# The stretch ahead of the main loop, put in another order: band, weights, conversion, gathers

## The chip, the cores and the metric

The kernel runs on one NeuronCore of a Trainium2 chip. The metric is the device time of one execution in microseconds (us). The time before is 1235.25 us, the median of three runs (1234.21 to 1237.3). The engines are named as in the profile: PE (TensorE, matmuls), PEld (its weight loads), DVE (VectorE), ACT (ScalarE), POOL (GpSimd) and SP (SyncE, which here only issues DMAs). ACT and POOL issue DMAs too, in the order of their own programs; the issuing parts are called SPq and ACTq in the trace.

## The reference

For x of shape (8, 4224, 192) in float32, cut to what matters:

```python
w = softmax(weight, axis=-1)                       # 8 heads x 7 taps
x = einsum('hk,bskhg->bshg', w, causal windows of x)   # a 7-tap convolution along the sequence
u = x + real(fft(fft(x, axis=1), axis=2))          # sequence 4224 = 33 * 128, features 192
un = (u - mean(u)) / sqrt(var(u) + 1e-6)           # over the 192 features
out = u + maximum(un @ w_ch1, 0) @ w_ch2           # 192 -> 768 -> 192, weights in float64
```

The two weight matrices arrive as 64-bit floats, so the kernel itself turns their 8-byte words into 32-bit floats.

## The kernel before, in words

**Values in two parts.** All large products are made of float16 pairs: a high part (ACT, one copy with a scale) and a low part (DVE, what is left). The scale of each operand is a power of two from its norm: ACT squares and sums, PE adds over the partitions (`pn`), ACT takes a root, DVE a reciprocal and a mask (`pow2_of_norm`).

**Stages of one batch.** (1) Convolution: PE multiplies windows `xt` of the input by a banded matrix `band` made from the taps (`conv_unit`, L472), ACT copies the result to `xa`, and DMAs store it to a scratch array `sc` in DRAM. (2) The rows come back from `sc` in another order as `xs` (for batch 0 by four indirect gathers on POOL, L572; later by plain DMAs) and are split into `XH` (ACT, L605 in batch 0) and `XL` (DVE, L612 in batch 0). (3) Stage A, a transform of length 128 (PE, L659, 16 tiles `pa`, each copied as `yh` by ACT, L667, and `yl` by DVE, L668). (4) Stage B, 33 by 3 (PE `pb`, L685; ACT and DVE make `V`, L693 and L694). (5) For each of nine groups of 512 rows (`it`), `prep`: the last transform (`pq`, L755), the row itself gathered into `xr` (`load_res`, L723, on POOL in batch 0), sum, mean and variance, `un`, its split `hl`, and a DMA transpose `kt`. (6) The MLP: `ph` (L892, six tiles), `hh` and `hlo` (ACT L896, DVE L897), `po` (L911, L914, L917), then the sum and the store.

**The loop and what stands ahead of it.** From `keep_order(tc)` on, a loop over 72 steps (8 batches of 9 groups) runs steps 5 and 6 and, as fill, stages 1 to 4 of the batches that follow. The change lies ahead of it, in about a hundred lines that carry batch 0 up to its first groups, make the convolution of batch 1, and prepare the weights. Each engine runs its instructions in the order in which they were recorded, so an instruction that waits holds all that stand behind it on that engine, DMA issues included.

**Names that the change touches.**
- `make_band`, `load_band` (L206 to L234): DVE works out the softmax of the taps, SP writes them as one row to DRAM (`line_d<-back`, L226), and reads it back shifted for each partition (`band_runs<-line_d`, L230); DVE copies it to `band` in eight pieces (L234). The first convolution matmul needs all of it.
- `load_group` (L493): an input chunk of batch 0 in two or three DMAs. Chunks 0 and 1 are issued by ACT; chunks 2 to 5 by SP.
- `from_float64` (L270 to L300): eight bytes to a float32, ten DVE instructions for each of four pieces: `w1a`, `w1c` (the first weight matrix W1) and `w2_0`, `w2_1` (the second, W2). `some(convs[k], n)` records the next n of them.
- `load_raw2(i)` (L323): loads half i of W2; half 0 into the memory of `XL`, half 1 (`raw_w2_1`) into a buffer of the tag `xs`, which is free once the first gathered piece is split.
- `high1`, `low1` (L371 to L388): W1's high parts on ACT (three instructions), its low parts on DVE (three, and two copies). `split2`: the same for W2. `square_w` (L342) and `pow2_of_norm`: their scales `s_w`.
- `c16_sb`: constants. `F` (128 columns twice) is used by stage A, `R` by stage B, `G` by `pq`.
- `gathers(k)`: four gathers on POOL of one group's rows into `xr`, of which there are three buffers.

## Time and profile before

| | us |
|---|---|
| three runs | 1234.21, 1237.3, 1235.25 |
| median | 1235.25 |
| the profiled execution | 1241.18 |
| its span, first to last instruction | 1239.4 |
| PE busy in the span | 1172.8 |
| first `ph` matmul on PE | 101.83 |

The profile is one execution, with its own time, which is 5.9 us above the median of the runs; durations come from it. Times in rows are counted from the span's start. A row of the time line gives start, length, engine, line, operation, output and input, shape, count, and in brackets how long the engine was idle before it and what ended that. A row of the groups gives line, engine, operation, shape and count, then busy time and mean length of one in ns, then the idle time before. A row of the table by windows gives the stretch, its length, the busy time and instruction count of PE, PEld, DVE, ACT and POOL, the granted PE clock (1.00 is full), the DMA share and GB/s. PE is busy for 95% of the span; the idle part lies for the most part ahead of 140 us.

### The profile page before, as it was taken

The page shows a single profiled execution, that of the slowest core. Times are in us where ns is not written, and L with a number is a line of the kernel's source. Part 1 is how long each engine was busy: PE and PEld are TensorE (multiplying, and loading weights), DVE is VectorE, ACT ScalarE, POOL GpSimd, SP SyncE. Part 2 cuts the span into 40 slices and gives each one's busy share as a digit, 9 for nine tenths or more (in the row PEclk, how much of TensorE's full clock was granted, in tenths as well). Part 3 has the DMA queues.
Part 4 walks back from the last instruction along what each step waited for, and adds up shares of the span by engine and source line. Part 5 has one row for each costly group of instructions (what it writes and reads, how often), then busy time and mean ns, then how long its engine had stood idle before and what let it go on. Part 6 is the DMA issues. An engine that isn't in the chain of part 4 may idle for free.

```text
span 1239.4 us, 30189 instructions
## 1 busy us (share of the span) xinstructions
PE 1172.8 (95%) x12234; PEld 933.0 (75%) x12234; DVE 807.2 (65%) x1998; ACT 818.6 (66%) x1581; POOL 501.1 (40%) x503
## 2 busy tenths in 40 slices
PE   5278899999999999999999999999999999999999
PEld 4276578787878878787877878788787867777777
DVE  4787575567666666667566676666865786556654
ACT  5476686678657876678656886578665676556542
POOL 2428233355244444445333552444443452346210
PEclk9599999999999999999999999999999999999999
DMA  8856784695435853486535754358452442323321
GB/s 261 316 149 150 163 207 133 171 215 149 108 100 155 211 139 79 120 204 174 136 93 157 190 149 109 96 150 207 108 126 78 122 90 68 78 68 87 74 53 46
DMA packets 225732, 170.14 MB, mean 137 GB/s; under 512 B 119151, under 2 KB 206925, under 8 KB 225592
## 3 DMA queue, kind: packets, MB, share of 16 engines
q1 hardware_dynamic: 212646, 141.03, 45.1%
q0 software_dynamic: 11136, 25.34, 7.0%
q8 instruction: 95, 1.56, 0.5%
q10 hardware_dynamic: 1810, 1.84, 0.5%
q14 instruction: 45, 0.37, 0.1%
HBM read 84.50 MB, written 58.50 MB: 115 GB/s over the span
## 4 chain that ended last, share of the span: by engine, by line
PE 78%; DVE 9%; ACT 5%; DMA 4%; issue 2%; another core or an unknown queue 1%; SPq 1%; POOL 1%; ACTq 0%; DVEq 0%
PE ph L892 30%; PE po L911 9%; PE po L917 9%; PE po L914 9%; PE pa L659 7%; PE pq L755 5%; PE pc L472 5%; PE pb L685 5%; DMA sc<-xa 2%; ACT un L835 1%; DVE XL L637 1%; DVE hlo L897 1%; ACT XH L633 1%; ACT hh L896 1%
## 5 line engine op out<-in xcount | busy, mean ns | idle before, releaser
L892 PE MATMUL ph<-kt,W 128*128 128x512 f16 (+1 forms) x2160 | 494.2, 362 | 9.9 <-DVE hlo L897 7.2
L897 DVE SCALAR_TENSOR_TENSOR hlo<-ph,hh 128x512 f16<-128x512 f32 (+1 forms) x400 | 271.1, 679 | 251.0 <-ACT hh L896 220.2
L896 ACT ACTIVATE hh<-ph 128x512 f16<-128x512 f32 (+1 forms) x400 | 237.2, 594 | 290.3 <-PE ph L892 266.9
L911 PE MATMUL po<-W,hh 128*128 128x192 f16 x1584 | 388.2, 246 | 2.7 <-ACT hh L896 1.7
L914 PE MATMUL po<-W,hh 128*128 128x192 f16 x1584 | 388.1, 246 | 2.2 <-DVE W L394 2.2
L917 PE MATMUL po<-W,hlo 128*128 128x192 f16 x1584 | 388.0, 247 | 1.5 <-DVE hlo L897 1.4
L892 PEld LDWEIGHTS <-W 128*128 128x128 f16 x2160 | 193.5, 98 | 153.1 <-issue 12.6
L791 POOL TENSOR_TENSOR u<-u,xr 128x768 f32<-128x768 f32 (+1 forms) x70 | 119.1, 1702 | 319.6 <-ACT u L790 286.1
L723 POOL DMA_INDIRECT xr<-sc,rows_sb x175 | 193.2, 1104 | 50.5 <-issue 34.8
L849 POOL TENSOR_TENSOR hl<-un,hl 128x512 f16<-128x512 f32 (+1 forms) x144 | 126.1, 898 | 145.9 <-ACT hl L846 120.4
L911 PEld LDWEIGHTS <-hh 128*128 128x128 f16 x1584 | 155.2, 98 | 19.7 <-ACT hh L896 2.2
L917 PEld LDWEIGHTS <-hlo 128*128 128x128 f16 x1584 | 154.9, 98 | 17.8 <-issue 2.6
L914 PEld LDWEIGHTS <-hh 128*128 128x128 f16 x1584 | 155.1, 98 | 16.4 <-issue 0.7
L668 DVE SCALAR_TENSOR_TENSOR yl<-pa,yh 99x512 f16<-99x512 f32 x128 | 86.6, 686 | 66.9 <-ACT yh L667 48.4
L835 ACT ACTIVATE un<-u,nm,y 128x192 f32<-128x192 f32 x256 | 119.5, 544 | 8.0 <-DVE nm L822 5.3
L659 PE MATMUL pa<-c_sb,XH 128*128 128x128 f16 x1024 | 105.5, 222 | 16.7 <-ACT XH L605 16.1
L472 PE MATMUL pc<-xt,band 128*120 128x144 f32 x756 | 109.3, 289 | 4.8 <-DVE V L694 3.4
L472 PEld LDWEIGHTS pc<-xt,band 128*120 128x120 f32 x756 | 100.4, 184 | 13.4 <-DVE V L694 3.8
L659 PEld LDWEIGHTS <-XH 128*128 128x128 f16 x1024 | 84.9, 104 | 28.4 <-ACT XH L605 16.2
L923 DVE SCALAR_TENSOR_TENSOR u<-po,fo,u 128x384 f32<-128x384 f32 (+1 forms) x136 | 80.6, 593 | 37.8 <-PE po L917 29.2
L637 DVE SCALAR_TENSOR_TENSOR XL<-xs,s_x,XH 128x768 f16<-128x768 f32 (+1 forms) x56 | 100.4, 1796 | 6.0 <-ACT XH L633 6.0
L755 PE MATMUL pq<-c_sb,V 128*128 128x130 f16 (+1 forms) x1440 | 96.6, 215 | 2.5 <-issue 2.5
(145 smaller groups left out, 1498.0 us busy)
## 6 DMA issues: line engine op xcount, KB each, us to landing
out_dram<-u SPq DMA_DIRECT2D x64, 384.0 KB
xt<-in_xw_dram SPq DMA_DIRECT2D x36, 576.0 KB
sc<-xa SPq DMA_DIRECT2D x33, 540.0 KB
xs<-sc SPq DMA_DIRECT2D x84, 192.0 KB
xs<-sc SPq DMA_DIRECT2D x28, 216.0 KB
xr<-sc SPq DMA_DIRECT2D x56, 96.0 KB
xt<-in_xv_dram SPq DMA_DIRECT2D x6, 504.0 KB
sc<-xa SPq DMA_DIRECT2D x6, 472.5 KB
```

The lines of the kernel that those rows point to most:

```text
L472: nc.tensor.matmul(pc[:WR, h - h0], band[:, h], xt[:, :, h * GRP : (h + 1) * GRP], start=True, stop=True,)
L659: nc.tensor.matmul(pa[:, i], x[:, at], F[:, l], start=(n == 0), stop=(n == 2))
L723: nc.gpsimd.indirect_dma_start(bt.xr[it][:, g], None, bt.sc[: S if b else 128 * LP], bass.IndirectOffsetOnAxis(ap=(rows_sb if b else lines ...
L755: nc.tensor.matmul(po, weights(v, ND * r + k3), rhs[:, 0] if it == Q0 else rhs, start=(r + n == 0), stop=(r == 1 and n == 2),)
L835: nc.scalar.activation(un[:, g], u[:, g], AF.Identity, bias=nm[:, g : g + 1], scale=y[:, g : g + 1],)
L849: nc.gpsimd.tensor_tensor(bl[:, :, o : o + n], un[:, :ng, f], hi[:, :, f], op=ALU.subtract)
L892: nc.tensor.matmul(ph[:, n], W1[:, w, ht * 128 : (ht + 1) * 128], kt[:, k], start=(i == 0), stop=(i == len(order) - 1),)
L896: anchor[0] = nc.scalar.activation(hh, ph, AF.Relu).ins
L897: anchor[1] = nc.vector.scalar_tensor_tensor(hlo, ph, 0.0, hh, op0=ALU.max, op1=ALU.subtract).ins
L911: nc.tensor.matmul(po[:, g % 2], hh[:, ht, tk], W2[:, ht, 0], start=(ht == 0), stop=False)
L914: nc.tensor.matmul(po[:, g % 2], hh[:, ht, tk], W2[:, ht, 1], start=False, stop=False)
L917: nc.tensor.matmul(po[:, g % 2], hlo[:, ht, tk], W2[:, ht, 0], start=False, stop=(ht == 5),)
```

## The change

What it does, all of it ahead of the loop:
- **Band.** Input chunk 2 is issued by ACT behind chunks 0 and 1; the load of `band_runs` follows directly on the store of its row on SP.
- **W2 and constants.** Half 0 of W2 and `F` are issued by ACT behind the last of its stores; half 1 of W2 now stands ahead of `R`, `G` and the row numbers, and all of these behind the fourth split on SP.
- **Conversion.** Eight DVE instructions in place of ten: the sign is kept by one combined instruction, and the last three bits of the low word are dropped by one shift.
- **W1.** `high1` and `low1` now stand ahead of the splits of batch 0, the pieces of the W2 conversion between the low parts; the square of W2's half 0 goes behind stage B.
- **Gathers.** The rows of group 2 are gathered with those of groups 0 and 1; those of group 3 in two pairs; the four of group 4 between these.
- **Order of the rest.** The conversion of `w2_1`, its norm, `split2` and the stages of `prep` of groups 0 and 1 are recorded earlier and mixed otherwise.

ACT, from its last stores to its splits; `sc` is the scratch array, `XL` here the landing place of half 0 of W2, `c_sb` the constants, `W` the split W1. Before:

```order
L959 DMA sc_173<-xa_5_287 112x2x192
L959 DMA sc_173<-xa_5_287 120x2x192
L255 ACTIVATE r_x_331<-r_x_331 128x1
L342 ACTIVATE sq_w_0_350,nrm_w_349<-w1a 128x768
L342 ACTIVATE sq_w_1_352,nrm_w_349<-w1c 128x384
L255 ACTIVATE r_w_361<-r_w_361 128x1
L605 ACTIVATE XH<-xs_0_341,s_x_335 128x2x432 x2
L605 ACTIVATE XH<-xs_1_343,s_x_335 128x2x384 x2
```

ACT at the same place, now:

```order
L955 DMA sc_173<-xa_5_285 112x2x192
L955 DMA sc_173<-xa_5_285 120x2x192
L326 DMA XL<-in_w_dram 128x3x384
L1090 DMA c_sb<-in_c_dram 128x256
L255 ACTIVATE r_x_327<-r_x_327 128x1
L338 ACTIVATE sq_w_0_346,nrm_w_345<-w1c 128x384
L338 ACTIVATE sq_w_1_348,nrm_w_345<-w1a 128x768
L255 ACTIVATE r_w_354<-r_w_354 128x1
L367 ACTIVATE W_78<-w1a,s_w_358 128x768
L370 ACTIVATE W_78<-w1c,s_w_358 64x384 x2
L601 ACTIVATE XH<-xs_0_337,s_x_331 128x2x432 x2
```

Two DMA issues stand ahead of the roots and squares now, and three copies of W1 ahead of the splits; before, those copies stood behind the last split.

DVE, from the scale of W1 to the first low split of batch 0 (`cv` are the buffers of the conversion, `w2f` its result). Before:

```order
L257 RECIPROCAL r_w_361<-r_w_361 128x1
L259 TENSOR_SCALAR s_w_368<-r_w_361 128x1
L262 TENSOR_SCALAR s_w_368<-s_w_368 128x1
L292 SCALAR_TENSOR_TENSOR XL<-XL,cv_w_0_315 128x576
L294 TENSOR_TENSOR cv_w_0_314<-cv_w_0_314,XL 128x576
L297 TENSOR_SCALAR cv_w_0_315<-XL 128x576
L299 SCALAR_TENSOR_TENSOR w2f<-cv_w_0_315,cv_w_0_314 128x576
L612 SCALAR_TENSOR_TENSOR XL<-xs_0_341,s_x_335,XH 128x432 x4
```

DVE at the same place, now:

```order
L262 TENSOR_SCALAR s_w_358<-s_w_358 128x1
L279 TENSOR_SCALAR cv_w_0_312<-XL 128x576
L281 SCALAR_TENSOR_TENSOR cv_w_0_312<-XL,cv_w_0_312 128x576
L285 TENSOR_SCALAR cv_w_0_313<-cv_w_0_312 128x576
L380 SCALAR_TENSOR_TENSOR W_78<-w1c,s_w_358,W_78 64x384
L384 COPY W_78<-W_78 64x2x384
...
L375 SCALAR_TENSOR_TENSOR W_78<-w1a,s_w_358,W_78 128x768
L291 TENSOR_TENSOR cv_w_0_312<-cv_w_0_312,XL 128x576
L293 TENSOR_SCALAR cv_w_0_313<-XL 128x576
L295 SCALAR_TENSOR_TENSOR w2f<-cv_w_0_313,cv_w_0_312 128x576
L608 SCALAR_TENSOR_TENSOR XL<-xs_0_337,s_x_331,XH 128x432 x4
```

Before, six of the ten conversion instructions stood ahead of the scale and four behind it; now the whole conversion and all low parts of W1 stand between the scale and the first split.

POOL, behind the first eight gathers of rows (`xr`, one row for each group of rows; `hl` is the split of `un`). Before:

```order
L849 TENSOR_TENSOR hl_0_870<-un_0_855,hl_0_870 128x4x64
L723 DMA xr_2_874<-sc_173,lines_sb 128x192 x4
L700 COPY V_0_708<-V_2_938 128x12x8
L849 TENSOR_TENSOR hl_1_970<-un_1_933,hl_1_970 128x4x128
L849 TENSOR_TENSOR hl_1_970<-un_1_933,hl_1_970 128x4x64
L723 DMA xr_3_974<-sc_173,lines_sb 128x192 x4
L723 DMA xr_4_1205<-sc_173,lines_sb 128x192 x4
L791 TENSOR_TENSOR u_2_1006<-u_2_1006,xr_2_874 128x768
```

POOL at the same place, now:

```order
L719 DMA xr_2_428<-sc_173,lines_sb 128x192 x4
L696 COPY V_0_709<-V_0_675 128x12x8
L696 COPY V_0_709<-V_1_711 128x12x8
L719 DMA xr_3_813<-sc_173,lines_sb 128x192 x2
L719 DMA xr_4_1197<-sc_173,lines_sb 128x192 x4
L845 ISA
L845 TENSOR_TENSOR hl_0_872<-un_0_862,hl_0_872 128x4x128
L845 TENSOR_TENSOR hl_0_872<-un_0_862,hl_0_872 128x4x64
L719 DMA xr_3_813<-sc_173,lines_sb 128x192 x2
L696 COPY V_0_709<-V_2_940 128x12x8
```

Group 2 is fetched ahead of stage B now, and the eight gathers that stood in one run behind `hl_1` are gone from there.

The diff, with the lines of smaller moves left out:

```diff
@@ from_float64
-        V.tensor_scalar(ai, hi_w, 30, 30, op0=SR, op1=SL)
         V.tensor_scalar(bi, hi_w, 5, 2, op0=SL, op1=SR)
-        V.tensor_tensor(bi, bi, ai, op=ALU.bitwise_or)
-        V.scalar_tensor_tensor(bi, lo_w, 29, bi, op0=SR, op1=ALU.bitwise_or)
-        V.tensor_scalar(lo_w, lo_w, 3, 3, op0=SL, op1=SR)
+        V.scalar_tensor_tensor(
+            bi, hi_w, 0xC0000000, bi, op0=ALU.bitwise_and, op1=ALU.bitwise_or
+        )
         V.tensor_scalar(ai, bi, 23, 23, op0=SR, op1=SL)
-        V.scalar_tensor_tensor(rem, lo_w, 2.0 ** -52, aux, op0=ALU.mult, op1=ALU.mult)
+        V.tensor_scalar(lo_w, lo_w, 1, None, op0=SR)
+        V.scalar_tensor_tensor(rem, lo_w, 2.0 ** -51, aux, op0=ALU.mult, op1=ALU.mult)
...
-    for ch in range(2):
+    for ch in range(3):
         load_group(first, ch, nc.scalar, *slots[ch])
     make_band()
-    load_group(first, 2, nc.sync, *slots[2])
+    load_band()
...
     for store in late:
         store()
-    load_raw2(0)
-    nc.sync.dma_start(c16_sb[:, n_r : n_r + n_f], c16[:, n_r : n_r + n_f])
+    load_raw2(0, nc.scalar)
+    nc.scalar.dma_start(c16_sb[:, n_r : n_r + n_f], c16[:, n_r : n_r + n_f])
...
     norm = pow2_of_norm(mlp["nw1"], 2, 11, "w1")
     next(norm)
+    next(norm)
+    mlp["s1"] = last(norm)
+    high1()
     some(convs[2], 3)
-    next(norm)
+    low1(0)
+    low1(1)
+    some(convs[2], 2)
+    low1(2)
     some(convs[2], 3)
-    mlp["s1"] = last(norm)
-    some(convs[2], 4)
...
         if n == 3:
+            load_raw2(1, nc.sync)
             nc.sync.dma_start(c16_sb[:, :n_r], c16[:, :n_r])
...
-            load_raw2(1)
...
     low()
-    high1()
-    square_w("w2", mlp["w2_0"], 0)
-    for f in gathers(0) + gathers(1):
+    for f in gathers(0) + gathers(1) + gathers(2):
         f()
...
+    square_w("w2", mlp["w2_0"], 0)
     chunk(second, 0)
     prep_piece(1)
+    prep_piece(0)
+    later = gathers(3)
+    for f in later[:2]:
+        f()
...
     total()
-    stage_b(first, 3)
-    some(half, 3)
-    chunk(second, 5)
-    stage_b(first, 4)
     square_w("w2", mlp["w2_1"], 1)
     norm = pow2_of_norm(mlp["nw2"], 2, 15, "w2")
+    stage_b(first, 3)
+    chunk(second, 5)
     next(norm)
+    stats.pop(0)()
+    stage_b(first, 4)
     next(norm)
+    mlp["s2"] = last(norm)
     for f in stats:
         f()
-    mlp["s2"] = last(norm)
```

More of the change, by code (lines that the diff above doesn't have):

```diff
@@ L277, in from_float64 @@
         bi, ai = bits.bitcast(U32), aux.bitcast(U32)
-        V.tensor_scalar(ai, hi_w, 30, 30, op0=SR, op1=SL)
-        yield
         V.tensor_scalar(bi, hi_w, 5, 2, op0=SL, op1=SR)
         yield
-        V.tensor_tensor(bi, bi, ai, op=ALU.bitwise_or)
-        yield
-        V.scalar_tensor_tensor(bi, lo_w, 29, bi, op0=SR, op1=ALU.bitwise_or)
-        yield
-        V.tensor_scalar(lo_w, lo_w, 3, 3, op0=SL, op1=SR)
+        V.scalar_tensor_tensor(
+            bi, hi_w, 0xC0000000, bi, op0=ALU.bitwise_and, op1=ALU.bitwise_or
+        )
         yield
@@ L291, in from_float64 @@
         yield
-        V.scalar_tensor_tensor(rem, lo_w, 2.0 ** -52, aux, op0=ALU.mult, op1=ALU.mult)
+        V.tensor_scalar(lo_w, lo_w, 1, None, op0=SR)
+        yield
+        V.scalar_tensor_tensor(rem, lo_w, 2.0 ** -51, aux, op0=ALU.mult, op1=ALU.mult)
         yield
@@ L321, in load_raw1, with load_raw2 @@
             )
-    def load_raw2(i):
+    def load_raw2(i, queue):
         w2v = w2.rearrange("(c p) e -> p c e", p=128)
@@ L329, in load_raw2 @@
             to = raw("w2_1", "xs", 3 * D)
-        nc.sync.dma_start(
+        queue.dma_start(
             to.rearrange("p (c e) -> p c e", c=3), w2v[:, 3 * i : 3 * i + 3]
@@ L1062 @@
     nc.sync.dma_start(wt, weight.rearrange("(o h) k -> o (h k)", o=1))
-    for ch in range(2):
+    for ch in range(3):
         load_group(first, ch, nc.scalar, *slots[ch])
     make_band()
-    load_group(first, 2, nc.sync, *slots[2])
+    load_band()
     nc.scalar.activation(cp.tile([128, 1], F32, name="warm"), eps, AF.Sqrt)
-    load_band()
     for ch in range(3, NCH):
@@ L1093 @@
         store()
-    load_raw2(0)
-    nc.sync.dma_start(c16_sb[:, n_r : n_r + n_f], c16[:, n_r : n_r + n_f])
+    load_raw2(0, nc.scalar)
+    nc.scalar.dma_start(c16_sb[:, n_r : n_r + n_f], c16[:, n_r : n_r + n_f])
     convs.append(convert("w2_0", 3 * D))
-    some(convs[1], 10)
     norm = scales(first)
+    some(convs[1], 4)
     next(norm)
+    some(convs[1], 4)
     next(norm)
@@ L1103 @@
         load_x(first, i)
-    square_w("w1", mlp["w1a"], 0)
-    square_w("w1", mlp["w1c"], 1)
+    square_w("w1", mlp["w1c"], 0)
+    square_w("w1", mlp["w1a"], 1)
     norm = pow2_of_norm(mlp["nw1"], 2, 11, "w1")
     next(norm)
+    next(norm)
+    mlp["s1"] = last(norm)
+    high1()
     some(convs[2], 3)
-    next(norm)
+    low1(0)
+    low1(1)
+    some(convs[2], 2)
+    low1(2)
     some(convs[2], 3)
-    mlp["s1"] = last(norm)
-    some(convs[2], 4)
     low = None
@@ L1144 @@
     prep_piece(1)
+    prep_piece(0)
     chunk(second, 1)
-    for _ in range(3):
-        prep_piece(0)
-    for part in range(2):
-        conv_unit(second, 2, part)
     prep_piece(0)
-    for f in gathers(2):
-        f()
-    conv_unit(second, 2, 2)
+    conv_unit(second, 2, 0)
+    prep_piece(0)
     transposes(first, 0)
-    for _ in range(2):
-        prep_piece(1)
-    for i in range(3):
-        low1(i)
     half = convert("w2_1", 3 * D)
-    chunk(second, 3)
+    some(half, 1)
     for _ in range(3):
         prep_piece(1)
+    for part in range(1, 3):
+        conv_unit(second, 2, part)
+    for f in later[2:]:
+        f()
+    some(half, 2)
+    prep_piece(1)
+    chunk(second, 3)
+    prep_piece(1)
     stage_b(first, 2)
     prep_piece(1)
-    for f in gathers(3):
-        f()
+    some(half, 2)
+    transposes(first, 1)
     some(half, 1)
-    transposes(first, 1)
-    some(half, 4)
     chunk(second, 4)
```

## The prediction

> **What bounds the kernel now.** I read the table by windows first: length, busy time and count of PE, PEld, DVE, ACT and POOL, granted PE clock, DMA share, GB/s.
>
> ```profile
> span 1239.4 us, 30189 instructions
> 13.94:40.51 26.57, 13.46 (x100) 12.84 (x100) 16.82 (x42) 13.39 (x30) 6.10 (x9) 0.81 0.90 284
> 40.51:53.88 13.37, 0.00 (x1) 0.01 (x1) 8.96 (x19) 5.61 (x7) 10.63 (x10) 0.50 0.86 312
> 53.88:70.12 16.24, 14.33 (x194) 13.75 (x194) 13.93 (x22) 13.45 (x23) 2.92 (x3) 0.88 0.64 247
> 70.12:101.83 31.71, 25.82 (x321) 24.64 (x322) 26.89 (x73) 23.80 (x51) 15.94 (x16) 0.95 0.66 164
> 101.83:122.44 20.61, 16.16 (x134) 11.05 (x134) 14.61 (x42) 12.00 (x28) 16.62 (x19) 0.92 0.58 153
> 122.44:140.00 17.56, 12.56 (x98) 8.11 (x96) 11.41 (x32) 9.21 (x14) 8.23 (x9) 0.99 0.48 99
> 140.00:1239.40 1099.40, 1086.97 (x11381) 859.52 (x11381) 709.34 (x1745) 735.87 (x1423) 440.44 (x435) 1.00 0.51 129
> ```
>
> From 140 on PE is idle for 1099.40 - 1086.97 = 12.4 us of 1099, so a shift of the loop's start arrives whole at the end, and nothing in the loop can repay more. Ahead of 140 PE is idle for 13.4 us while batch 0 is fetched and split (40.51 to 53.88), then 1.9, 5.9, 4.5 and 5.0 us in the next windows. The change can only act there.
>
> The time line next (start, length, engine, line, operation, and the idle time before with what ended it) gives the order of events up to the first matmul with a low part:
>
> ```profile
> 6.95 0.84 SPq L493 DMA_DIRECT2D xt<-in_xw_dram  x2
> 7.83 0.42 SPq L230 DMA_DIRECT2D band_runs<-line_d  x1
> 13.62 1.53 DVE L234 COPY band<-band_runs 128x120 f32<-128x120 f32 x8 [6.96 <-DMA band_runs<-line_d]
> 31.75 3.27 ACTq L959 DMA_DIRECT2D sc<-xa  x2
> 35.25 0.20 ACT L255 ACTIVATE r_x<-r_x 128x1 f32<-128x1 f32 x1 [5.67 <-DVE r_x L254]
> 37.56 0.46 DVE L279 TENSOR_SCALAR cv_w<-XL 128x576 uint32<-128x576 uint32 x1 [0.46 <-DMA XL<-in_w_dram]
> 40.51 1.22 POOL L572 DMA_INDIRECT xs<-sc,lines_sb  x1 [11.26 <-DVE cv_w L285]
> 43.15 0.76 DVE L299 SCALAR_TENSOR_TENSOR w2f<-cv_w,cv_w 128x576 f32<-128x576 uint32 x1
> 46.86 2.41 DVE L612 SCALAR_TENSOR_TENSOR XL<-xs,s_x,XH 128x432 f16<-128x432 f32 x4 [2.95 <-ACT XH L605]
> 54.53 0.33 PE L659 MATMUL pa<-c_sb,XL 128*128 128x128 f16 x1 [0.22 <-DVE XL L612]
> ```
>
> The gather comes at 40.51, DVE waits 2.95 us for the first high part, and PE starts when the low parts are there. The releaser printed for the gather, a DVE line, had long been done; what ends that wait is a DMA, the last store.
>
> **The change, part by part.** *Band.* Two issues (0.84 us) leave SP ahead of the band's load, and chunk 2's data flows earlier, while the DMA engines are nearly idle:
>
> ```profile
> 6.00:8.00 2.00, 0.00 (x0) 0.00 (x0) 0.59 (x3) 1.77 (x3) 0.00 (x0) 1.00 0.19 61
> ```
>
> The band load takes 13.62 - 7.83 = 5.8 us from issue to first copy, behind chunk 2's transfer. At the lower bound it gains nothing (DMA full anyway: 0.90 up to 40.51), at the upper 0.84 plus some 1.4 of that queueing, -2.2. I take -1.0, nearest to the issue row.
>
> *Last stores and gather.* W2's half 0 and F go behind the last stores on ACT. Of the window before the gather at most the stretch from W2's landing can be saved, 40.51 - 37.56 = 2.95, and the band's 1.0 to 2.2 with it: -1 to -5; I take -4. The first high split would come 4 us earlier with it, but that does not set the end any more, because DVE has other work then.
>
> *DVE ahead of the low splits.* The conversion of half 0 ran from 37.56 to 43.91. Two kinds of instruction go from it:
>
> ```profile
> L283 DVE TENSOR_TENSOR cv_w<-cv_w,cv_w 128x576 uint32<-128x576 uint32 x1 | 0.8, 757 | 0.0
> L281 DVE TENSOR_SCALAR cv_w<-XL 128x576 uint32<-128x576 uint32 x1 | 0.5, 451 | 0.0
> ```
>
> That is 1.2 us; without the scale's three small ones (0.5) it is 6.35 - 0.5 - 1.2 = 4.7 us. The low parts of W1, five instructions, come from the stretch behind stage B:
>
> ```profile
> 84.51 0.74 DVE L384 SCALAR_TENSOR_TENSOR W<-w1c,s_w,W 64x384 f16<-64x384 f32 x1
> 87.10 1.02 DVE L379 SCALAR_TENSOR_TENSOR W<-w1a,s_w,W 128x768 f16<-128x768 f32 x1
> L612 DVE SCALAR_TENSOR_TENSOR XL<-xs,s_x,XH 128x384 f16<-128x384 f32 (+1 forms) x16 | 8.9, 626 | 4.3 <-ACT XH L605 4.3
> ```
>
> From 84.51 to 87.10 + 1.02 they take 3.6 us. So DVE has 4.7 + 3.6 = 8.3 us of work ahead of its first low split, from the landing of W2 and the scale of W1 on. Both I put near 37.6: W2 is issued about 2 us later than before but with less in its way; the scale needs ACT's root (35.25), which now stands behind two more DMA issues but behind a shorter wait for the stores (3.27 in the row). First low split: 37.6 + 8.3 = 45.9, before 46.86. Eleven splits of 0.626 (6.9 us) lead to the first matmul with a low part: 52.8 to 53.0 in place of 54.53. **Term 1: -1.5.** If W2 lands a microsecond earlier or later, so does all of this: bounds -3 to +4 (the third rival). The 2.4 us that W1's own two conversions lose count for nothing: ACT's root and squares cover them, being held by the issues; without that cover they would add to the gain.
>
> *ACT in stage A.* ACT made W1's high parts and a square between its last split and the first `yh`:
>
> ```profile
> 55.39 0.92 ACT L371 ACTIVATE W<-w1a,s_w 128x768 f16<-128x768 f32 x1
> 57.47 0.69 ACT L342 ACTIVATE sq_w<-w2f 128x576 bf16<-128x576 f32 x1
> 58.15 2.04 ACT L667 ACTIVATE yh<-pa 99x512 f16<-99x512 f32 x4
> 58.76 11.31 DVE L668 SCALAR_TENSOR_TENSOR yl<-pa,yh 99x512 f16<-99x512 f32 x16 [1.64 <-ACT yh L667]
> ```
>
> These 2.8 us are gone from there. DVE's sixteen `yl`, 11.31 us without a gap, then set the end of stage A; the 1.64 us that they waited can go, but DVE itself comes free only at 45.9 + 16 x 0.626 = 55.9 and behind that needs a first `yh`. I take half a microsecond beyond term 1. **Term 2: -0.5**, bounds 0 to -1.6.
>
> *Gathers on POOL.* Group 2's four go ahead of stage B, where POOL is busy for 2.92 of 16.24 us: nothing. Six more stand ahead of `hl_0` now, behind which all of group 0 waits.
>
> ```profile
> L723 POOL DMA_INDIRECT xr<-sc,rows_sb x175 | 193.2, 1104 | 50.5 <-issue 34.8
> 83.68 2.10 POOL L849 TENSOR_TENSOR hl<-un,hl 128x512 f16<-128x512 f32 x2 [9.58 <-ACT hl L846]
> ```
>
> Six at 1.1 us and 0.3 of issue are 8.4 us; POOL was idle for 9.58 there. I count nothing, with +0.5 as a bound, since four of them also wait for group 1's sum to free their buffer.
>
> *From stage B to the first `ph`.* DVE sheds the 3.6 us of low parts, two instructions of W2's second half, one of them slow there, and a wait:
>
> ```profile
> L283 DVE TENSOR_TENSOR cv_w<-cv_w,cv_w 128x576 uint32<-128x576 uint32 x1 | 1.6, 1598 | 0.0
> 80.66 0.18 DVE L817 RECIPROCAL y<-sd 128x4 f32<-128x4 f32 x1 [1.63 <-ACT sd L813]
> ```
>
> That is 3.6 + 1.6 + 0.5 + 1.6 = 7.3 us of 31.71, but DVE is idle for 31.71 - 26.89 = 4.8 us there, PE for 5.9, and ACT's 23.80 us, conversion copies among them, are neither shorter nor better placed. **Term 3: -2**, between 0 (ACT holds the pace) and -5.9 (all idle time of PE).
>
> *W2 ready earlier.* PE waits once for W2's low part, and the clock falls behind that; a like wait stands ahead of a convolution.
>
> ```profile
> 90.81 0.75 PE L472 MATMUL pc<-xt,band 128*120 128x144 f32 x4 [3.07 <-DVE V L694]
> 90.00:95.00 5.00, 4.19 (x47) 4.17 (x48) 4.90 (x8) 4.62 (x10) 4.53 (x6) 0.70 0.54 158
> 116.00 0.32 PE L914 MATMUL po<-W,hh 128*128 128x192 f16 x1 [2.17 <-DVE W L394]
> 115.00:120.00 5.00, 4.00 (x24) 3.34 (x24) 4.76 (x9) 2.32 (x6) 3.75 (x5) 0.66 0.25 60
> ```
>
> The conversion and the norm of the second half are recorded earlier, so the 2.17 us go, and with them part of the loss at 0.66 (5 us at full clock would do 1.7 us more; I take half). **Term 4: -3**, bounds 0 (W2 is late in another place) and -3.9. The Trainium skill ("TensorE: Matmul & The Clock Gate", Part 1: The HAM clock gate) speaks against the second half of this: the clock halves only after an idle window of about 3.4 us, so a gap of 2.17 would cost no clock. The trace shows 0.66 behind it, and 0.70 behind a gap of 3.07, both shorter than the page's window. By the page term 4 would be -2.2 and the sum 0.8 smaller; I go by the rows.
>
> Sum: -1.5 - 0.5 - 2 - 3 = -7.0. Against the profiled execution's own 1241.18 us (span 1239.4 and 1.8 around it) that is 1234.2. That execution lies 5.9 us above the median of the runs, so I subtract from the median: 1235.25 - 7.0 = 1228.2, said as **1228**.
>
> **Rivals.** *First: it gives more.* The chain of waits has two steps that no engine explains:
>
> ```profile
> 102.56 4.00 another core or an unknown queue
> 125.04 4.96 another core or an unknown queue
> ```
>
> In both, POOL is amid eight gathers in a row. Nowhere else in the run do eight stand together, and the change parts them. If the gathers make these stalls, what PE still loses there goes too: 4.5 - 2.2 (term 4) in 101.83 to 122.44 and 5.0 up to 140, in all 7.3, which gives 1235.25 - 14.3 = 1221. Against it: the profiled execution was 5.9 us above the median, so the stalls may be a matter of that execution alone. Chance 0.18.
>
> *Second: the gain is hidden.* The order of transfers changes little, W2 decides as late as before, and what is shed behind stage B was cover for ACT's copies (23.80 of 31.71) and for PE's waits on PSUM. Then terms 1 and 2 stand with -2 and the rest gives nothing: 1233, within 0.3% (3.7 us, about what a measurement of this kernel can tell from no change). That the whole does not do what it says, because the band's row and not its load is late, ends here as well. For it: ACT has no more slack than DVE. Against: the wait of 2.17 names W2. Chance 0.20.
>
> *Third: slower, W2's half 0 lands late.* It stands behind ACT's last stores, whose issue ended at 31.75 + 3.27 = 35.0, and the conversion and all low parts of W1 stand behind it ahead of every low split.
>
> ```profile
> 31.34 6.20 DMA XL<-in_w_dram
> 45.15 7.72 DMA xs<-sc,lines_sb
> ```
>
> Before, it took 6.20 us; beside gathers, which took up to 7.72, it would land at 35.0 + 7.7 = 42.7, and the first low split would start at 42.7 + 8.3 = 51.0, +4.2. With half a microsecond won by ACT stage A ends 3.7 us later; half 1 of W2 stands on SP behind the fourth split and is late with it, so terms 3 and 4 give nothing: 1235.25 + 3.7 = 1239. It decides from a landing later than 46.86 - 8.3 = 38.5 on. Against it: fewer bytes are ahead of the stores than before, so they should end sooner than 35.0. Chance 0.12.
>
> **How the numbers follow.** My own case has 0.50, with -4 to -10 (1225 to 1231). With the first rival that makes 0.68 for faster by over 0.3%; the second gives 0.20 for no change, the third 0.12 for slower. The range for 8 in 10 reaches from 1219 (the first rival with its bounds) to 1236 (the second with +0.5 on POOL and a term 1 of nothing), which leaves out the third rival and the tails.
>
> **What would show it.** Right: band copies near 11.7 to 12.6 in place of 13.62; the gather at 36 to 38; conversion from about 37.6 and the first low split at about 45.9; the first matmul with a low part at 53; `yl` without the 1.64 us of idle time; no wait for `W` near 116 and a clock above 0.66 behind it; first `ph` near 98, and 7 us off at the point that was 140. Wrong: W2 landing past 38.5, DVE waiting ahead of its conversion, POOL's `hl_0` behind a gather, or PE as idle between 70 and 122 as before. If the two stalls of 4.00 and 4.96 us are gone and the time is near 1221, the first rival holds.

## The result, and the profile after

| | before | after |
|---|---|---|
| median, us | 1235.25 (7 runs, 1233.18 to 1237.30) | 1224.65 (7 runs, 1221.33 to 1229.70) |
| ratio to before | 1 | 0.9924 (95%: 0.9908 to 0.9940) |
| profiled execution: its time, its span | 1241.18, 1239.4 | 1224.36, 1222.5 |
| first matmul with a low part | 54.53 | 51.88 |
| first `pb` (stage B) | 69.40 | 66.31 |
| first `ph` | 101.83 | 96.03 |
| first output store issued | 134.13 | 120.05 |

The change saves 10.6 us by the medians, 0.6 to 0.9% by the interval; 7.0 were forecast. The two profiled executions differ by 16.8, more than the medians, because that of before lay 5.9 above its own median. In the rows of after all line numbers behind the conversion are 4 lower (L608 is the low split that was L612). Its table by windows, cut at the same events as before (band, gather, first `pa`, second row of `pb`, first `ph`, and 125.92, which answers to 140):

```profile
13.42:37.50 24.08, 13.46 (x100) 12.84 (x100) 11.74 (x33) 13.49 (x30) 6.50 (x9) 0.82 0.89 298
37.50:50.62 13.12, 0.00 (x0) 0.00 (x0) 12.80 (x25) 7.65 (x10) 10.58 (x9) 0.50 0.80 279
50.62:67.03 16.41, 14.46 (x194) 13.95 (x194) 14.81 (x24) 11.18 (x18) 10.15 (x7) 0.84 0.88 330
67.03:96.03 29.00, 24.57 (x273) 23.64 (x274) 23.74 (x68) 23.32 (x50) 18.27 (x19) 0.90 0.70 182
96.03:125.92 29.89, 29.78 (x300) 22.18 (x298) 25.31 (x70) 24.86 (x50) 18.82 (x21) 0.99 0.71 184
125.92:1222.50 1096.58, 1083.64 (x11363) 857.88 (x11360) 710.88 (x1747) 735.33 (x1418) 439.49 (x435) 1.00 0.51 128
```

PE's 13.4 us without work while batch 0 is fetched and split are still there (13.12), only sooner. From stage B to the first `ph` PE is idle for 4.4 us in place of 5.9. The large difference is the stretch behind the first `ph`: 0.1 us of idle time, before 4.5 and 5.0 in its two windows. The first events, from the time line:

```profile
13.10 1.51 DVE L234 COPY band<-band_runs 128x120 f32<-128x120 f32 x8 [6.45 <-DMA band_runs<-line_d]
32.45 0.41 ACTq L326 DMA_DIRECT2D XL<-in_w_dram  x1
37.50 1.07 POOL L568 DMA_INDIRECT xs<-sc,lines_sb  x1 [7.51 <-DMA XL<-in_w_dram]
37.99 0.46 DVE L279 TENSOR_SCALAR cv_w<-XL 128x576 uint32<-128x576 uint32 x1
45.02 0.78 DVE L295 SCALAR_TENSOR_TENSOR w2f<-cv_w,cv_w 128x576 f32<-128x576 uint32 x1
45.73 8.74 DVE L608 SCALAR_TENSOR_TENSOR XL<-xs,s_x,XH 128x432 f16<-128x432 f32 x16
51.88 0.33 PE L655 MATMUL pa<-c_sb,XL 128*128 128x128 f16 x1 [0.82 <-DVE XL L608]
```

From 37.99 on DVE has no idle time at all: 7.7 us of conversion and low parts, then sixteen low splits in 8.74 without a gap, where before they came in three pieces and waited for ACT.

```profile
53.53 0.61 ACT L663 ACTIVATE yh<-pa 99x512 f16<-99x512 f32 x1 [1.30 <-DVE XL L608]
57.27 9.71 DVE L664 SCALAR_TENSOR_TENSOR yl<-pa,yh 99x512 f16<-99x512 f32 x13 [0.19 <-ACT yh L663]
```

ACT is free before there is anything to copy in stage A (1.30 us idle); the copies of W1 that stood there are gone. For the end of W2's preparation, POOL's sum of group 2 and W2's high part on ACT, and then PE's longest waits between 60 and 140 (view of the waits: in all, times, longest):

```profile
90.30 2.43 POOL L787 TENSOR_TENSOR u<-u,xr 128x768 f32<-128x768 f32 x1 [0.35 <-ACT u L786]
101.18 0.77 ACT L389 ACTIVATE W<-w2f,s_w 128x576 f16<-128x576 f32 x1
```

```profile
PE pc L468 <- ACT XH L473: 2.1, 1, 2.1
PE pc L468 <- DVE V L690: 1.8, 1, 1.8
```

No wait for `W` is left, and no stretch that no engine explains.

### The profile page after: what moved, and what is told of

Same layout as the page of the kernel before. It is cut to its first block, busy times and chain, and to the rows that moved or that the text cites. A ratio compares the mean times of both kernels' runs of the same rounds, so it can differ in the third digit from the quotient of the medians.

```text
span 1222.5 us, 30180 instructions
## 1 busy us (share of the span) xinstructions
PE 1169.4 (96%) x12234; PEld 933.6 (76%) x12234; DVE 804.6 (66%) x1990; ACT 821.0 (67%) x1581; POOL 504.0 (41%) x503
## 4 chain that ended last, share of the span: by engine, by line
PE 82%; DVE 7%; ACT 4%; DMA 4%; issue 2%; POOL 1%; SPq 0%; ACTq 0%; DVEq 0%
PE ph L888 31%; PE po L907 9%; PE po L913 9%; PE po L910 9%; PE pa L655 7%; PE pc L468 6%; PE pq L751 5%; PE pb L681 5%; ACT un L831 1%; DVE XL L633 1%; DMA sc<-xa 1%; DMA xt<-in_xw_dram 1%; DVE hlo L893 1%; ACT XH L629 1%; ACT hh L892 1%
## 5 line engine op out<-in xcount | busy, mean ns | idle before, releaser
L719 POOL DMA_INDIRECT xr<-sc,rows_sb x175 | 193.2, 1104 | 50.5 <-issue 34.8
L655 PE MATMUL pa<-c_sb,XL 128*128 128x128 f16 x512 | 95.3, 221 | 0.8 <-DVE XL L608 0.8
```

What stands on the lines that cost most here:

```text
L655: nc.tensor.matmul(pa[:, i], x[:, at], F[:, l], start=(n == 0), stop=(n == 2))
L719: nc.gpsimd.indirect_dma_start(bt.xr[it][:, g], None, bt.sc[: S if b else 128 * LP], bass.IndirectOffsetOnAxis(ap=(rows_sb if b else lines ...
```

## The experiments

Twelve kernels in three sets of four. The sets ran on three different chips, each with its own runs of before beside it (medians 1235.77, 1234.36 and 1241.66 us), so ratios are compared, not times. After has its own ratio from the result above and ran beside none of the sets. The events are from one profile of each kernel, and one profile says only so much: e7 and e12 have after's order behind stage B, yet take 31.6 and 30.1 us from `pb` to `ph` where after takes 29.7, so differences of up to 2 us in that column decide nothing. "Store" is the first output store. The expectations give 70.12 as the first `pb` of before, which is its second row; the first is at 69.40. The order in which an engine runs comes out of a scheduler that starts from the recorded one (so `xr_4`, recorded in the loop, stands between the two pairs of `xr_3`), and an edit can move more than its own lines.

| run | median us | ratio (95%) | first low matmul | first `pb` | `pb` to `ph` | `ph` to store |
|---|---|---|---|---|---|---|
| before | 1235.25 | 1 | 54.53 | 69.40 | 32.4 | 32.3 |
| after | 1224.65 | 0.9924 (0.9908 to 0.9940) | 51.88 | 66.31 | 29.7 | 24.0 |
| e1_front | 1231.42 | 0.9963 (0.9950 to 0.9977) | 53.95 | 68.31 | 31.9 | 29.3 |
| e2_tail | 1231.39 | 0.9963 (0.9947 to 0.9978) | 54.34 | 69.19 | 33.0 | 23.6 |
| e3_gathers | 1233.78 | 0.9982 (0.9969 to 0.9995) | 52.98 | 67.85 | 35.1 | 24.7 |
| e4_gathers_back | 1230.44 | 0.9952 (0.9937 to 0.9967) | 53.06 | 68.08 | 28.5 | 28.8 |
| e5_gathers_back_stats | 1228.63 | 0.9951 (0.9934 to 0.9968) | 52.02 | 67.04 | 28.5 | 25.6 |
| e6_w1_back | 1229.46 | 0.9961 (0.9948 to 0.9975) | 51.44 | 66.00 | 35.2 | 24.8 |
| e7_w2_sync | 1226.54 | 0.9943 (0.9922 to 0.9964) | 52.25 | 67.15 | 31.6 | 25.1 |
| e8_tail_full | 1235.81 | 1.0018 (1.0003 to 1.0033) | 56.53 | 71.37 | 37.5 | 24.9 |
| e9_root_later | 1236.43 | 0.9947 (0.9931 to 0.9962) | 53.10 | 73.21 | 31.9 | 24.3 |
| e10_w1_back_root_later | 1236.82 | 0.9948 (0.9929 to 0.9967) | 52.78 | 71.37 | 32.3 | 24.9 |
| e11_ten_instructions | 1238.36 | 0.9963 (0.9948 to 0.9979) | 53.49 | 72.99 | 33.0 | 24.7 |
| e12_band_back | 1237.56 | 0.9957 (0.9934 to 0.9980) | 54.57 | 75.03 | 30.1 | 24.5 |

**The front alone.** After up to the end of stage A, before behind it; group 2's gathers stand behind stage A again:

```diff
-    for f in gathers(0) + gathers(1) + gathers(2):
+    for f in gathers(0) + gathers(1):
...
     for t in range(NT):
         stage_a(first, t)
-    (the order of after, from stage_b(first, 0) to split2)
+    (the order of before, without its low1(i))
```

> The changed kernel up to the end of stage A; from stage B to the loop the order of before (gathers in two runs of eight again, second half of W2 converted late), except that W1's low parts stay ahead of the splits. Marks: first matmul with a low part 54.53 before, 51.88 after; first pb 70.12 and 66.31; first ph 101.83 and 96.24; first output store 134.13 and 120.05. Theory (each stage's own work decides): the first two marks as after, first ph about 98 (DVE has lost 3.6 us of low parts and 1.2 us of conversion behind stage B, the order has not changed), and from first ph to first store again about 32 us, so 5 to 6 us below before. Rival (gathers in a row make the stalls, and little else counts): the early lead is eaten by the same stalls, 3 us below before or less. Rival (hidden gain: ACT's copies hold the pace behind stage B): first ph no more than 3 us earlier, total 2 to 3 us below before.

Measured: 4.4 us below before, between the theory (5 to 6) and its two rivals (up to 3); the first `ph` at 100.19 is where the last rival put it. Less came of the first stretch than in the profile of after, because ACT stood longer at its last stores, and W2 with it:

```profile
28.96 6.36 ACTq L955 DMA_DIRECT2D sc<-xa  x4
35.35 0.45 ACTq L326 DMA_DIRECT2D XL<-in_w_dram  x1
47.80 8.74 DVE L608 SCALAR_TENSOR_TENSOR XL<-xs,s_x,XH 128x432 f16<-128x432 f32 x16
```

W2 was issued at 35.35, the conversion began at 40.08, right behind the late scale of W1, and the first low split came at 47.80, 0.9 later than before's. The rest did not follow it: stage B still began 1.1 us sooner than before, since the sixteen splits ran without a gap and `yl` behind them. From `pb` to `ph` half a microsecond is won: 3.6 us fewer on DVE buy nearly nothing there in the old order. From `ph` to the first store it takes 29.3 although POOL has both runs of eight gathers, and there is no unexplained stretch.

**The tail alone.** Before up to stage A, the order of after behind it (W1's low parts stay on DVE there). This kernel leaves out the last two of the ten conversion instructions of W2's second half.

```diff
-    for f in gathers(0) + gathers(1):
+    for f in gathers(0) + gathers(1) + gathers(2):
...
-    (the order of before from stage_b(first, 0) to split2)
+    (the order of after, with low1(i) ahead of convert("w2_1"))
```

> The kernel before up to the end of stage A, but with group 2's gathers ahead of it; behind stage B the order of after (gathers of group 3 in pairs, second half of W2 converted and its norm taken earlier), with W1's low parts still on DVE there. Theory: the first two marks as before (54.5 and 70.1, at most 0.5 off), first ph 0 to 2 us earlier, from first ph to first store about 26 us in place of 32, total 4 to 6 us below before. Rival (gathers parted): first ph to first store as short as after (24), total 6 to 8 below. Rival (W1's low parts on DVE take back what the order gives): total within 2 us of before.

4.4 us below before, and `ph` to the first store as short as after (23.6). But with the two instructions in place it is another picture:

> The second run once more (the kernel before up to stage A, the order of after behind it), now with all ten conversion instructions of W2's second half; the second run left out the last two of them, 1.2 us of DVE. Theory: 0 to 1.5 us above that run's 1231.4, so 3 to 4 us below before, with the long wait of PE for a convolution buffer (6.9 us there) again, because DVE's low parts of W1 stand ahead of what frees it. Rival (the order alone carries the gain): 1228 or less.

Measured: 0.2% slower than before. The last stretch is again short (24.9), but from `pb` to `ph` it takes 37.5 us in place of 32.4, and this profile was 2 us late at the first low matmul already (ACT's last stores took 5.80 us there). So the new order alone is no gain. Both kernels have the wait of 6.9 us for a convolution buffer that the theory names. The ratios of e2 and e8 are nearly 7 us apart, and two instructions explain a part: the last of them takes 2.28 us in e8, beside POOL's sum of group 2 (0.76 in after), which with the other makes 2.7 us of DVE, and PE's wait for the `V` behind it is 3.4 us there, 0.7 in e2. The rest stays open.

**The gathers alone, in before and in after.**

```diff
 (e3: before)
-    for f in gathers(0) + gathers(1):
+    for f in gathers(0) + gathers(1) + gathers(2):
...
+    later = gathers(3)
+    for f in later[:2]:
...
-    for f in gathers(2):
-    for f in gathers(3):
+    for f in later[2:]:
```

> The kernel before, with nothing but the gathers moved: group 2's ahead of stage A, group 3's in two pairs; on POOL no eight gathers stand in a row any more behind the first twelve. Theory (W2's order makes the gain, the stalls of 4.00 and 4.96 us belong to single executions): within 2 us of before, PE's wait of 2.2 us for W2's low part is still there. Rival (eight gathers in a row make the stalls): 5 to 8 us below before, and no wait of 3 us or more that no engine explains.

> The changed kernel, with nothing but the gathers put back: group 2's behind the first split of un, group 3's in one piece, so that one run of eight stands on POOL behind hl of group 1. Theory: within 2 us of after. Rival (runs of eight make the stalls): 4 to 7 us slower than after, with a wait of 4 us or so on ACT and DVE that no engine explains while the eight run.

Moved alone they win 2 us; put back in after they cost 3.5 (ratios 0.9952 and 0.9924, whose intervals overlap by a hair). Both lie between the forecasts: e3 at the edge of the theory, e4 short of the rival's 4 to 7. In e3 PE has no wait for `W` left, against the theory, although the conversion and the norm of W2 stand where before has them. The rival's mechanism is not there either: in e4 eight gathers stand in a row and there is no stretch that no engine explains. From its time line, POOL, DVE and ACT:

```profile
100.36 0.94 POOL L719 DMA_INDIRECT xr<-sc,lines_sb  x1 [0.30 <-issue]
101.33 1.83 POOL L787 TENSOR_TENSOR u<-u,xr 128x768 f32<-128x768 f32 x1
103.19 0.36 DVE L794 BATCH_NORM_STATS2 st<-u 128x6 f32<-128x192 f32 x1 [1.69 <-POOL u L787]
108.04 0.78 ACT L389 ACTIVATE W<-w2f,s_w 128x576 f16<-128x576 f32 x1
```

The sum of group 2 stands on POOL behind the eight gathers (101.33, after 90.30). Its statistics on DVE wait for it (1.69 us at 103.19), and behind them on DVE stand the scale of W2 and its low parts; W2's high part comes at 108.04, after at 101.18. DVE goes on in this order:

```profile
103.68 0.33 DVE L794 BATCH_NORM_STATS2 st<-u 128x6 f32<-128x192 f32 x1
105.00 0.17 DVE L795 BATCH_NORM_AGGREGATE mv<-st 128x2 f32<-128x6 f32 x1
106.05 0.15 DVE L254 TENSOR_SCALAR r_w<-pn_w 128x1 f32<-128x1 f32 x1
107.65 0.15 DVE L262 TENSOR_SCALAR s_w<-s_w 128x1 f32<-128x1 f32 x1
```

The statistics of group 2 (`st`, `mv`) come ahead of `r_w`, DVE's first step of W2's scale, and of the scale `s_w` itself, so W2 waits for a sum that it does not need. Before has these statistics ahead of W2's scale as well (behind `r_w`), and its wait of 2.17 us for `W`; after has them there too, but the sum is early.

**The same, with the statistics out of W2's way.**

```diff
 (e4, and:)
     next(norm)
-    stats.pop(0)()
...
-    for f in stats:
-        f()
     for i in range(2):
         split2(i)
     output_scale()
+    for f in stats:
+        f()
```

> The run with the gathers put back, and group 2's statistics moved on DVE from ahead of the scale and the low parts of W2 to behind them. In the run before it, POOL's sum of group 2 stood behind eight gathers and ended near 103, DVE waited 4.66 us ahead of its hlo at 99.62 and 1.69 us for the sum, and W2's high part came at 108.04 in place of 101.18 after. Theory (gathers cost through what is queued behind them: sum of group 2 on POOL, its statistics on DVE, and W2's scale behind these): W2's copy near 102 and the first po near 105 again, total at least 2 us below the run with the gathers put back, within 2 us of after. Rival (the gathers themselves, by their transfers or descriptors, slow the other engines): the first po stays near 110 and the total near the run with the gathers put back, 5 us above after.

The theory's mechanism came out: W2's high part at 101.65 and first store 25.6 behind the first `ph`. Its total did not: the ratio is that of e4. The late sum of group 2 is paid one place further on, ACT first, then PE:

```profile
101.65 0.77 ACT L389 ACTIVATE W<-w2f,s_w 128x576 f16<-128x576 f32 x1
125.06 1.86 ACT L831 ACTIVATE un<-u,nm,y 128x192 f32<-128x192 f32 x4 [4.86 <-POOL hl L845]
127.45 0.34 PE L907 MATMUL po<-W,hh 128*128 128x192 f16 x1 [3.95 <-ACT hh L892]
```

ACT waits 4.86 us until POOL has come through its queue, and `hh` stands behind that, so PE waits 3.95. So the gathers must be out of the way of POOL's sums and splits, wherever these are used.

**W1 back behind the splits.**

```diff
-    high1()
-    some(convs[2], 3)
-    low1(0)
...
+    some(convs[2], 8)
...
     low()
+    high1()
...
+    for i in range(3):
+        low1(i)
     half = convert("w2_1", 3 * D)
```

> The changed kernel, with W1's high parts on ACT again behind the last split and its low parts on DVE behind the first transposes, as before. Theory: DVE's first low split starts 2 to 3 us earlier, when the first high part is there (near 43), but the first matmul with a low part hardly moves, since the last high parts are not there before 51; ACT's 2.2 us come again between the splits and the first yh (+1 us at the first pb), and the 3.6 us of DVE work stand again between stage B and the first ph: first ph 2 to 4 us later, total 2 to 4 us above after. Rival (W1 first is neutral, it only fills idle time that DVE has anyway): within 1 us of after. Rival (W1 first costs more at the splits than it saves): 1 to 3 us below after.

4.6 us above after by the ratios. The first stretch does not suffer: the first low split comes at 44.19, and the first low matmul and `pb` are even 0.3 to 0.4 sooner than after (the theory had `pb` 1 us later). The loss is 5.5 us between `pb` and `ph`, more than the 2 to 4 expected, and its mechanism is in the rows of three engines (DVE, ACT, PE):

```profile
79.88 1.07 DVE L375 SCALAR_TENSOR_TENSOR W<-w1a,s_w,W 128x768 f16<-128x768 f32 x1
80.88 2.26 DVE L279 TENSOR_SCALAR cv_w<-raw_w 128x576 uint32<-128x576 uint32 x1
85.04 0.30 ACT L809 ACTIVATE sd<-mv,eps 128x4 f32<-128x4 f32 x1 [6.23 <-DVE mv L795]
85.80 1.32 PE L468 MATMUL pc<-xt,band 128*120 128x144 f32 x4 [6.92 <-ACT XH L473]
```

DVE does W1's low parts, an instruction of the conversion that takes 2.26 us there (0.45 in after, where a later one behind these statistics takes 2.09), and only then group 1's mean and variance; ACT's root of group 1 waits 6.23 us for these; the convolution's copies stand behind the root on ACT; PE waits 6.92 us for a buffer. The new order of ACT (root ahead of copies) holds only if DVE is free, and W1 first is what frees it. e2 and e8, with W1's low parts at the same place, show the same wait of 6.9 us, and after is without it. It does not explain all that parts these kernels: e2 wins 4.4 us with it.

**Root behind the copies**, in after (e9) and with W1 back (e10):

```diff
-    some(half, 1)
-    for _ in range(3):
-        prep_piece(1)
     for part in range(1, 3):
         conv_unit(second, 2, part)
+    for _ in range(3):
+        prep_piece(1)
+    some(half, 1)
```

> The changed kernel, with the last two convolution units of chunk 2 recorded ahead of the last three pieces of group 1, and the first instruction of W2's second conversion behind them: on ACT the root of group 1 (L809) then stands behind two copies and the square of chunk 2, not ahead of them. After: PE waits 2.09 us at 81.29 for a copy of this chunk, and the clock falls to half for 3.4 us behind that. Theory (ACT waits for group 1's mean and variance, and holds the convolution copies behind it): that wait of PE is below 1 us, the copies come 1.3 us earlier, and the total is 1 to 4 us below after (ratio to before 0.989 to 0.992). Rival (group 1's own chain sets the pace: the root comes 0.7 us later): the total is 0 to 2 us above after (0.9925 to 0.994).

> The run with W1's parts put back (0.9961 of before; PE waits 6.92 us there for a convolution copy, behind a root for which ACT waits 6.23 us), with the same two moves as the run beside it: the root of group 1 stands behind the copies of chunk 2. Theory (W1 first pays because its low parts on DVE held this root, and the root the copies): PE's wait of 6.92 us shrinks to less than 2, first ph 2 to 4 us earlier than 101.2, ratio to before 0.992 to 0.994. Rival (3.6 us of DVE work there are on the path in any order): ratio 0.9955 to 0.997, first ph near 101.

All four kernels of this set lost 4 to 6 us in stage A (last section), so their first `ph` and their ratios say little, and `pb` to `ph` is compared. PE's waits, of e10 and of e9:

```profile
PE pb L681 <- ACT XH L473: 3.0, 1, 3.0
```

```profile
PE pc L468 <- DVE V L690: 6.2, 2, 3.6
```

In e10 the wait of 6.92 is gone, and 3.0 is the longest left for a copy of ACT, more than the 2 expected; `pb` to `ph` is 32.3 in place of 35.2, the theory's 2 to 4 us. Its ratio (0.9948) lies between the two forecasts. In e9 no wait for a copy above 0.4 us is left, but PE waits 6.2 us for DVE's `V` in place of after's 1.8, and `pb` to `ph` became 31.9, 2.2 longer than after. That is the rival's side, but it is not the order alone. One instruction of DVE is slow in e9 and not in after; POOL's sum of group 2 and this instruction, first in e9, then after's:

```profile
97.56 1.95 POOL L787 TENSOR_TENSOR u<-u,xr 128x768 f32<-128x768 f32 x1
97.88 2.24 DVE L295 SCALAR_TENSOR_TENSOR raw_w<-cv_w,cv_w 128x576 f32<-128x576 uint32 x1
90.30 0.76 DVE L295 SCALAR_TENSOR_TENSOR raw_w<-cv_w,cv_w 128x576 f32<-128x576 uint32 x1
```

In after the two start together at 90.30, and it is POOL's that is long (2.43). In e9, e10, e6 and e7 POOL starts first, by 0.2 to 0.3 us, and DVE's takes 2.24 or 2.25. e7, with after's order there, so loses as much (31.6, and 4.3 us of waits for `V`) as e9. Whether the root's place costs or gains anything is therefore not shown. No kernel of this study has a lower ratio than after; of this set that decides nothing, as after was not run beside it.

**W2 on SP, ten instructions, band.**

```diff
 (e7)
-    load_raw2(0, nc.scalar)
-    nc.scalar.dma_start(c16_sb[:, n_r : n_r + n_f], ...
+    load_raw2(0, nc.sync)
+    nc.sync.dma_start(c16_sb[:, n_r : n_r + n_f], ...
 (e11: from_float64 of before, ten steps; e12: chunk 2 on SP between store and load of the band)
```

> The changed kernel, with half 0 of W2 and F issued by SP again, ahead of the last stores' end, as before. Theory (576 KB and the constants stand in the way of the last stores): the first gather is 1 to 3 us later than after's 37.50, W2's conversion does not start later, and the first low split moves by less than 1 us, since DVE's 8 us ahead of it hang on the scale; total 0 to 2 us above after. Rival (W2 behind the stores comes late): W2 is earlier here, first low split near 44, total 1 to 2 us below after. Rival (the gather decides): the first high part is 2 to 3 us later, and the total 2 to 3 us above after.

The gather came at 37.94, no later than in the kernels with W2 on ACT (37.50 to 38.77), and the first low split at 44.61, where the rival put it. The total can't be told from after's. So W2's new place does not move the gather, in one profile each.

> The changed kernel with the conversion of before, ten instructions for each piece. Theory (1.2 us more ahead of the low splits and as much again between stage B and the first ph): first low split near 47 in place of 45.73, first matmul with a low part up to 1 us later, first ph 1 to 3 us later, ratio to before 0.993 to 0.9955. Rival (DVE has the time): within 1 us of after, 0.9916 to 0.993.

```profile
47.30 8.77 DVE L612 SCALAR_TENSOR_TENSOR XL<-xs,s_x,XH 128x432 f16<-128x432 f32 x16
```

First low split at 47.30, with 9.0 us of DVE work ahead of it in place of 7.7, and 33.0 from `pb` to `ph`, 3.3 more than after and 1.4 more than e7. The ratio 0.9963 is just above the theory's bound, with the disturbance of this set in it. The work in the first place is shown; the first matmul with a low part, at 53.49, and the total cannot be told from those of e9, e10 and e12, so what the two instructions cost the whole is not. (The one shift of the new conversion drops only the last bit of the low word; its first three bits go with the rest of that word and no longer into the high one.)

> The changed kernel with the band's load behind input chunk 2 on SP, as before. In the profiles so far the band's copies on DVE start between 12.2 and 13.1 with the change and between 12.9 and 13.6 without. Theory: copies near 13.3, first low split 0 to 1 us later, ratio to before 0.992 to 0.994. Rival (the band sets the first stretch, and all shifts with it): 1 us and more later everywhere, ratio above 0.994. Rival (nothing): 0.9915 to 0.9925.

The band's copies began at 13.07, within the spread, but the gather came at 40.38 and the first low matmul 1.1 to 1.8 us after those of the other three of its set: nearest to the second case, though the copies moved by far less than a microsecond and the ratio's interval (0.9934 to 0.9980) takes in the first as well. It excludes the last. Over all profiles the copies start at 12.56 on average with the band changed (9 profiles) and at 13.21 without (5), the gather at 38.1 and 40.4.

## Why the prediction was right, and where not

The range of 1219 to 1236 around the forecast of 1228 held 1224.65. My own case of -4 to -10 just missed -10.6, and the range reaches so far down only for the first rival's sake: that it held is in part luck. By its steps:

- **Band, -1.0:** -0.65 at the copies (13.10 in after's profile, not the 11.7 to 12.6 given as a sign). But what follows is more than that: the gather's 2.3 us go with the band (e12 gives them back, e7 does not). How half a microsecond becomes two, no run shows.
- **Last stores and gather, -4:** -2.3, and not for the reason given: W2 and F behind the stores give nothing there (e7).
- **Term 1, -1.5:** after's profile has -2.65. The five profiles with this front unchanged (after, e1, e4, e5, e9) have 51.88 to 53.95, mean 52.8; the four with that of before (before, e2, e3, e8) 52.98 to 56.53, mean 54.6: -1.8. DVE's 8.3 us of work came out as 7.7. Behind it I misread a row: 626 ns is the length of one split, but they overlap, and 8.9 us busy for sixteen is 0.56 each. Eleven are 6.1 us, not 6.9 (6.15 in after), which by my own sum gives 52.0 and -2.5. The third rival's condition was met in e4 and e9, where DVE waits for W2 until 39.16 and 39.11 (against 38.5), without its price: the first matmul with a low part still came 1.4 us sooner than before, as the splits then ran without a gap.
- **Term 2, -0.5:** 69.40 - 54.53 = 14.87 before, 66.31 - 51.88 = 14.43 after: -0.4.
- **Term 3, -2:** -2.7 (e12 and e7, with the same order there, -2.4 and -0.8). The forecast took it as DVE's shed work, bounded by ACT; e1 has this shed work in the old order and wins 0.5. The rest goes with the new order, and only with W1 out of the way (e6, e8); which of its moves it is was not parted further.
- **Gathers at nothing:** here the working failed. Six gathers ahead of `hl_0` are not free: POOL's idle time was measured in the order of before, and `hl_0` behind a gather, which I gave as a sign of being wrong, came. `hl_0` in after, then in e4, where the gathers are put back:

```profile
81.35 1.80 POOL L845 TENSOR_TENSOR hl<-un,hl 128x512 f16<-128x512 f32 x2
80.79 1.78 POOL L845 TENSOR_TENSOR hl<-un,hl 128x512 f16<-128x512 f32 x2 [8.01 <-ACT hl L842]
```

From the first `pb` that is 15.0 us in after and 12.7 in e4; after stands right behind the last of the six. In e3 `pb` to `ph` grows by 2.6, and after takes 1.2 longer there than e4. And gathers are not only a matter of POOL's idle time: put back, they cost 4.8 us between `ph` and the first store (28.8 in e4, 24.0 after).

- **Term 4, -3, "W2 ready earlier":** the step that was mis-sized, with the wrong cause. From `ph` to the first store 29.3 (e1, which has no unexplained stretch) became 24.0: -5.3. Of that the earlier conversion and norm of W2's second half give 0.5 (e4 against e1: 28.8 and 29.3); the rest are the gathers, which held the sum of group 2, its statistics, and W2's scale behind them: e3, with nothing but the gathers moved, has 24.7. PE's wait for `W` alone would mislead here: it is 3.1 in e1, 0.5 in e4 and none in e3. The row of the 2.17 us named the last producer, `W` on DVE, and I asked what makes W, not what stands ahead of it in DVE's queue.
- **First rival:** right about the place, the gathers, and about more gain than 7; its mechanism is not shown. In e1, e4 and e5 eight gathers stand in a row without an unexplained stretch. The two stretches belong to the profiled execution of before, which needs 3.0 us more from `ph` to the first store than e1 with the same order of gathers.
- **The clock.** I went by the rows, and not by the rule quoted beside them. The rows hold, as the last section shows.

The sum in the new sizes: -1.8 - 0.4 - 2.7 - 5.3 = -10.2, measured -10.6. That they agree proves little, since the sizes come from different pairs of profiles, means for term 1 and e1 in place of before for term 4. What is left open: most of what parts e2 and e8, and where the loop's own spread comes from (from first to last store 1097 to 1104 us over these kernels, with the same instructions).

## What to carry to other kernels

A wait is printed with its last producer; before that producer is hurried, read what stands ahead of it in its own engine's queue, and in the queue of whoever feeds that. A long queue of transfers on one engine costs nothing by its length but by what it makes late behind it: keep short, needed work ahead of gathers that only prefetch. And an order that puts a waiting step ahead of other work pays only if its producer is early, so such a change must be judged together with what frees the producer. Last, before a difference between two profiles is put down to an edit, look for a kernel whose order is the same there and see how far that one differs.

## What the runs showed of the hardware

**PE's clock halves for windows of 3.41 us, and not only behind an idle one.** In every profile the stretches at half clock last 3.41 us or a multiple of it (but for one cut off by the end), and lie on a grid of that step. Two pairs of neighbouring windows of after (length, PE busy, ..., granted clock; laid to within 0.2 us of the grid):

```profile
79.70:83.10 3.40, 1.30 (x16) 1.17 (x17) 3.26 (x7) 2.58 (x7) 2.99 (x4) 1.00 0.89 284
83.10:86.50 3.40, 3.35 (x22) 3.35 (x22) 3.19 (x11) 3.40 (x8) 1.99 (x3) 0.52 0.81 130
89.90:93.30 3.40, 1.64 (x13) 1.36 (x12) 2.03 (x4) 2.47 (x8) 2.78 (x3) 1.00 1.00 240
93.30:96.70 3.40, 3.40 (x32) 3.03 (x32) 1.68 (x7) 2.68 (x6) 2.57 (x3) 0.52 0.93 231
```

A window in which PE was busy for 1.30 or 1.64 us is followed by one at half clock. The same in before, ahead of its half-clock windows, and one that was not followed by half clock:

```profile
88.54:91.95 3.41, 1.14 (x14) 1.11 (x15) 3.27 (x10) 1.64 (x4) 2.79 (x5) 1.00 1.05 267
112.43:115.84 3.41, 1.40 (x10) 0.67 (x8) 3.31 (x6) 3.05 (x7) 2.87 (x3) 1.00 0.21 58
85.10:88.50 3.40, 2.24 (x24) 2.01 (x23) 3.24 (x8) 3.21 (x8) 2.94 (x3) 1.00 0.95 181
```

So here no fully idle window is needed: with 1.64 of 3.40 us busy, 3.4 us at half clock followed, which by that length is a loss of up to 1.7 us. The busy time alone does not decide it. On the grid of each profile, from 12 us on, every full-clock window with less than 1.44 us busy was followed by half clock and none with more than 1.93, but between them both occur: 1.44 in e7 (from 139.35) by full clock, 1.93 in e11 (from 60.28) by half. A wait of 2 us that falls inside one window can cost this on top of itself. The Trainium skill ("TensorE: Matmul & The Clock Gate", Part 1: The HAM clock gate) gives the same window of about 3.4 us, but asks for a window of idleness; the measurement decides.

**A stretch in which PE is supplied slowly.** In all four kernels of the third set stage A took 18.6 to 20.5 us from first low matmul to `pb`, in place of 14.4 to 15.0. PE of e12 in this stretch, and one of POOL's gathers beside it:

```profile
63.89 0.34 PE L655 MATMUL pa<-c_sb,XH 128*128 128x128 f16 x2 [0.50 <-issue]
65.31 0.37 PE L655 MATMUL pa<-c_sb,XH 128*128 128x128 f16 x2 [1.01 <-issue]
66.03 0.27 PE L655 MATMUL pa<-c_sb,XH 128*128 128x128 f16 x1 [0.25 <-issue]
66.74 0.33 PE L655 MATMUL pa<-c_sb,XH 128*128 128x128 f16 x1 [0.44 <-issue]
64.56 0.95 POOL L719 DMA_INDIRECT xr<-sc,lines_sb  x1 [0.30 <-issue]
```

PE does two matmuls, then waits up to 1 us for nothing that the profile shows, and ACT and DVE wait for PE. It looks like the two stretches in the profile of before, and as there POOL is late in a long run of gathers. But the first two sets have runs of twelve and of eight without it. The four with it all ran on the third chip, where before is 6 to 7 us slower than on the other two; neither before nor after was profiled there, so the chip is as good a suspect as the gathers. What sets it off stays open.
